# More and narrower filler products, and a new order of all steps, in a fused attention and gated MLP kernel

## The chip, the cores and the metric

The kernel runs on one core of a Trainium2 chip. The metric is the device time of one execution in microseconds; several executions are timed and their median is given. One more execution is recorded by the hardware profiler, and every row shown here comes from that one.

## The reference

For 8 batches of 576 tokens and 8 heads of 64, attention keeps only the scores within `tau` of the row's maximum; the 8 heads are then joined to 512 columns and pass a gated MLP whose gate mixes tokens.

```python
scores = scale * np.matmul(q, k.transpose(0, 1, 3, 2))
thresh = np.max(scores, axis=-1, keepdims=True) - tau
scores = np.where(scores >= thresh, scores, -1000000000.0)
attn = np.exp(scores - np.max(scores, axis=-1, keepdims=True))
attn = attn / (np.sum(attn, axis=-1, keepdims=True) + 1e-09)
x = (attn @ v)                      # heads side by side: (B, S, 512)
...
h = gelu_tanh(x @ w_in)             # (B, S, 1024)
u, v = h[..., :512], h[..., 512:]
v_n = (v - mean(v)) / np.sqrt(var(v) + 1e-06) * g_ln
v_s = np.einsum('ts,bsd->btd', w_sg, v_n) + b_sg[None, :, None]
return x + (u * v_s) @ w_out
```

## The kernel before

The work is cut into 32 attention units `n` (a batch and two heads each; four units make a batch) and 8 MLP units. All inputs are float32; the MLP's products are made of high and low parts, three products for each, so TensorE (PE) has most of the work.

An attention unit loads `rq`, `rk` and `rv`, scales `rq` on GpSimd (POOL), and makes scores for four blocks of 128 queries and a tail of 64 (`scores`, 16 PE records for a block; `tail_scores`). A block fills two pairs of PSUM banks, one for each head. VectorE (DVE) takes the row maximum, POOL the threshold, ScalarE (ACT) the selection (`select`, which frees the banks) and the exponential (`exponentials`); DVE transposes blocks of 32 (`turn_blocks`), and DMAs issued by SyncE (SP) write them to DRAM tiles `swa` and `swb` and read them back into `pt` (`put_blocks`, `get_blocks`). PE then multiplies by `rv` (`values`), and the result becomes `x`. Once a batch has its four `x` tiles, its MLP runs between the attention of the units that follow.

The first batch has no MLP of an earlier batch beside it. In this opening the weights are also prepared: the words of `w_in` and `w_out` come as float64 and are turned into high and low parts by ACT, POOL, DVE and, for six of them, PE (`rest`, three products with 512 columns).

Each step of all this is entered into a list, `plan`. What the engines get is `plan` in the order of the table `ORDER`, a list of step numbers that is written out in the file. Every engine then works through its own instructions in that order. `PLACES` is a second table: one digit for each request of PSUM banks, in the order of the requests.

`warm_up` is a step without use for the result: it multiplies a tile of ones by itself into a PSUM bank that nobody reads.

Of the kernel before, what the change touches and what calls it, by code (L numbers as in the profile page):

```python
# [12 lines left out]
F32 = mybir.dt.float32  # L13
# [18 lines left out]
    172 16 17 173 18 174 65 250 7 1 14 71 188 19 178 189 190 66 191 76 179 180 67 176 68 195 192 69 181 175 196 182  # L32
    204 70 206 205 193 183 185 77 12 4 194 197 207 72 251 211 214 98 208 252 87 215 216 253 217 78 73 224 186 209 184
    225 5 221 218 74 266 79 226 187 10 88 212 54 80 227 75 222 99 213 267 210 9 15 219 268 223 228 89 100 32 21 220 43
    139 198 150 229 82 256 236 269 273 270 257 258 282 55 199 90 259 81 200 237 91 177 238 44 263 328 283 83 254 101
    284 260 231 285 274 203 230 46 84 93 286 232 289 261 292 239 330 329 85 102 293 92 294 201 302 332 295 103 303 262
    202 271 299 275 86 234 233 94 235 13 3 109 296 241 300 406 264 304 95 331 240 297 305 272 334 96 45 244 104 306
    245 242 128 49 335 336 265 56 97 287 337 338 290 11 105 6 344 341 307 298 301 291 243 339 276 278 22 60 407 112
    110 106 288 277 246 346 345 409 107 408 314 308 247 38 360 347 248 249 281 309 362 361 47 310 280 315 255 57 348
    351 380 8 349 363 108 316 340 381 317 342 350 382 113 367 370 383 364 343 352 371 372 279 412 410 114 373 111 353  # L40
    313 115 312 33 374 413 377 414 415 320 58 422 311 355 318 416 375 368 116 384 419 118 321 59 378 365 423 48 424
    117 425 61 322 376 323 369 739 385 379 426 366 319 2 324 62 35 417 420 429 325 50 741 354 356 134 392 121 448 421
    450 449 327 51 27 393 386 451 388 326 34 119 394 455 418 452 387 52 458 430 124 427 456 358 459 333 460 438 359
    395 120 428 440 740 24 156 461 125 0 439 441 23 357 431 122 36 445 442 63 126 37 390 462 446 25 389 745 746 391
    747 432 26 123 748 400 396 397 398 749 443 742 399 453 743 752 28 39 463 457 401 447 444 127 755 151 64 454 29 40
    470 402 434 433 153 145 756 753 152 757 53 129 464 403 471 30 140 758 466 762 791 465 41 759 405 404 31 771 472
    154 772 411 773 42 437 155 131 130 792 435 774 473 501 750 778 436 760 467 761 793 468 775 142 794 484 781 469 132
    776 133 475 474 795 478 476 783 763 782 157 477 764 479 784 502 583 135 785 788 754 751 779 136 141 789 158 780
    786 480 817 518 481 485 787 796 161 482 159 160 790 137 803 584 486 777 503 487 895 488 765 767 766 20 504 505 489
    490 506 804 818 491 492 138 493 567 519 568 520 507 494 534 819 495 521 522 496 483 508 509 523 497 510 535 823  # L50
    799 797 591 511 498 162 536 575 499 824 825 512 826 744 770 513 514 143 805 500 827 515 830 592 537 524 164 585
    525 768 769 569 833 526 538 798 516 806 800 527 810 539 576 550 528 529 586 834 835 517 570 809 540 551 577 530
    144 541 167 531 836 163 828 571 532 533 837 165 572 840 802 801 552 553 573 896 146 542 543 554 807 811 574 899
    544 578 545 587 555 808 812 588 599 556 546 557 813 558 147 559 613 589 841 822 579 580 849 547 831 148 560 820
    614 590 561 581 548 851 582 593 562 600 897 838 850 594 563 606 549 821 839 852 595 596 853 856 601 615 607 608
    829 832 898 564 597 859 565 598 842 566 844 843 634 860 861 635 854 814 609 857 616 862 845 636 610 617 866 602
    863 858 855 869 603 815 149 637 870 867 901 871 864 902 620 903 621 166 872 904 873 638 865 622 908 627 905 623
    628 816 624 629 847 618 630 639 604 874 973 848 975 168 169 605 868 911 912 913 170 611 914 641 881 882 642 883
    648 906 649 612 846 877 875 650 876 640 631 625 643 884 918 880 915 619 626 907 651 171 927 632 655 652 633 929
    656 662 919 916 644 878 653 928 654 657 909 658 663 664 887 879 910 930 974 947 917 931 934 886 937 920 948 645  # L60
    976 977 949 923 665 939 888 938 935 676 666 885 659 677 950 940 921 667 646 941 944 1300 889 936 979 647 890 945
    932 942 668 922 981 980 946 678 933 697 982 660 983 986 951 989 891 943 1025 892 679 926 1302 952 900 990 991 698
    690 893 984 987 699 1026 691 985 992 1027 993 996 1028 959 988 894 661 953 700 955 1005 960 692 997 683 1029 994
    954 961 701 925 924 1007 1006 680 1301 1008 684 669 962 670 671 693 1009 995 998 1012 958 681 1304 1015 1010 694
    672 957 967 956 1016 1017 999 966 1013 1000 1018 704 1303 685 1001 1014 1030 686 702 1019 1022 968 963 1306 965
# [989 lines left out]
```

## Time and profile before

| | |
|---|---|
| median of 3 executions | 855.63 us |
| the three | 855.70, 855.63, 844.68 us |
| the profiled execution | 844.72 us, its span 842.9 us |
| granted TensorE clock, mean over the span | 0.996 of full |
| busy share | PE 96%, ACT 77%, DVE 74%, POOL 57% |

The span runs from the first to the last instruction; 1.8 us of the profiled execution lie around it. Busy time of PE is modelled, since its products overlap. A granted clock of 1.0 is the 2.4 GHz level, 0.5 the 1.2 GHz level.

### The profile page before, as it was taken

How to read it: one execution, taken by the hardware profiler on the slowest of the kernel's cores; microseconds unless marked ns; L12 is line 12 of the kernel's file. 1: busy time of each engine (PE TensorE's matmuls, PEld its weight loads, DVE VectorE, ACT ScalarE, POOL GpSimd, SP SyncE). 2: the span in 40 equal slices, each digit the busy share in tenths (PEclk: the TensorE clock that was granted, in tenths of full speed). 3: DMA queues.
4: the chain of work that ended last, by engine and by line, in shares of the span. 5: the costliest groups of instructions: out<-in, count | busy, mean ns of one | idle time of the engine just before them, and what ended most of it. 6: DMA issues, size and time to landing. Idle time of an engine off the chain costs nothing.

```text
span 842.9 us, 24738 instructions
## 1 busy us (share of the span) xinstructions
PE 808.5 (96%) x9726; PEld 661.7 (78%) x9726; DVE 625.0 (74%) x1118; ACT 644.8 (77%) x1358; POOL 479.8 (57%) x809
## 2 busy tenths in 40 slices
PE   7779989999999999999999999999999999999898
PEld 4445767887888778888888878878788878889798
DVE  6888788858878487875788678874987748876265
ACT  6988879858979488786888678884898759886271
POOL 4788798544754477254753557334665348435283
PEclk9999999999999999999999999999999999999999
DMA  7998865784678735996558836797377853877402
GB/s 283 261 278 225 230 154 144 203 231 136 147 205 223 188 105 153 239 247 151 149 160 221 228 100 132 212 255 208 109 186 203 215 144 94 210 198 188 106 8 71
DMA packets 218998, 151.74 MB, mean 180 GB/s; under 512 B 32257, under 2 KB 204289, under 8 KB 218882
## 3 DMA queue, kind: packets, MB, share of 16 engines
q1 hardware_dynamic: 218882, 150.16, 67.0%
q8 instruction: 76, 1.25, 0.6%
q14 instruction: 40, 0.33, 0.1%
HBM read 97.68 MB, written 52.43 MB: 178 GB/s over the span
## 4 chain that ended last, share of the span: by engine, by line
PE 55%; DMA 16%; POOL 9%; SPq 6%; DVE 5%; ACT 5%; issue 3%; DVEq 0%; POOLq 0%; ACTq 0%
PE all_banks L759 33%; PE all_banks L552 11%; PE all_banks L667 9%; DMA pt<-swb 4%; DMA swb<-pt 4%; PE all_banks L559 2%; DMA ir<-ird 2%; SPq L646 2%; DVE pt L636 2%; SPq L653 2%; DVE columns L568 2%; DMA swa<-pt 2%; DMA rq<-in_qT 1%; DMA out_T<-ot 1%; ACT p L582 1%
## 5 line engine op out<-in xcount | busy, mean ns | idle before, releaser
L568 DVE TENSOR_REDUCE columns<-all_banks 128x1 f32<-128x576 f32 x288 | 205.6, 748 | 69.2 <-PE all_banks L552 48.7
L582 ACT ACTIVATE p<-all_banks,columns 128x576 f32<-128x576 f32 x288 | 201.5, 736 | 58.4 <-POOL columns L572 57.9
L588 ACT ACTIVATE p<-p,columns 128x576 f32<-128x576 f32 x288 | 221.0, 772 | 0.9
L636 DVE STREAM_TRANSPOSE pt<-p 128x576 f32<-128x576 f32 x288 | 209.0, 756 | 13.1 <-ACT p L588 7.6
L552 PE MATMUL all_banks<-rk,rq 64*64 64x288 f32 x2048 | 167.1, 417 | 11.5 <-ACT p L582 8.6
L667 PE MATMUL all_banks<-pt,rv 64*64 64x128 f32 (+1 forms) x4608 | 156.0, 284 | 7.8 <-DMA pt<-swb 4.3
L667 PEld LDWEIGHTS all_banks<-pt,rv 64*64 64x64 f32 x4608 | 144.7, 133 | 18.3 <-DMA pt<-swb 5.1
L572 POOL TENSOR_TENSOR columns<-columns 128x2 f32<-128x2 f32 (+1 forms) x160 | 34.1, 213 | 173.0 <-DVE columns L568 160.9
L552 PEld LDWEIGHTS all_banks<-rk,rq 64*64 64x64 f32 x2048 | 77.9, 133 | 64.3 <-ACT p L582 23.3
L759 PE MATMUL all_banks<-x,wi 128*128 128x288 f32 (+2 forms) x720 | 114.6, 300 | 0.0
L759 PE MATMUL all_banks<-wi,x 128*128 128x512 f32 (+1 forms) x424 | 110.4, 398 | 3.7 <-ACT ot L976 2.8
L759 PE MATMUL all_banks<-wsh,z 128*128 128x288 f32 (+2 forms) x512 | 112.2, 302 | 0.6 <-POOL z L880 0.6
L967 POOL TENSOR_TENSOR ot<-ot,x 128x288 f32<-128x288 f32 x112 | 89.9, 805 | 39.5 <-ACT ot L976 34.7
L759 PEld LDWEIGHTS all_banks<-x,wi 128*128 128x128 f32 x720 | 101.1, 188 | 13.6 <-issue 9.2
L759 PE MATMUL all_banks<-gh,wo 128*128 128x288 f32 (+1 forms) x480 | 107.7, 301 | 1.4 <-DVE ir L677 1.2
L759 PEld LDWEIGHTS all_banks<-wi,x 128*128 128x128 f32 (+1 forms) x424 | 74.2, 184 | 23.6 <-ACT ot L976 3.0
L759 PEld LDWEIGHTS all_banks<-wsh,z 128*128 128x128 f32 x512 | 83.4, 188 | 11.1 <-issue 6.4
L759 PEld LDWEIGHTS all_banks<-gh,wo 128*128 128x128 f32 x480 | 79.5, 188 | 14.5 <-issue 5.3
L759 PE MATMUL all_banks<-wsl,z 128*128 128x288 f32 (+2 forms) x256 | 74.4, 299 | 0.0
L685 POOL TENSOR_TENSOR x<-ir,x 128x576 fp32r<-128x576 f32 x32 | 45.6, 1424 | 42.8 <-ACT x L682 39.2
L759 PE MATMUL all_banks<-gl,wo 128*128 128x288 f32 (+1 forms) x240 | 69.7, 295 | 0.0
L675 DVE TENSOR_TENSOR ir<-all_banks,ir 128x512 f32<-128x512 f32 x32 | 21.7, 677 | 50.6 <-PE all_banks L667 38.8
(163 smaller groups left out, 1151.5 us busy)
## 6 DMA issues: line engine op xcount, KB each, us to landing
rv<-in_vP SPq DMA_DIRECT2D x32, 576.0 KB, 5.4
swb<-pt SPq DMA_DIRECT2D x64, 180.0 KB, 3.9
swb<-pt SPq DMA_DIRECT2D x32, 360.0 KB, 4.0
pt<-swb SPq DMA_DIRECT2D x64, 180.0 KB, 4.8
pt<-swb SPq DMA_DIRECT2D x32, 360.0 KB, 5.7
rq<-in_qT SPq DMA_DIRECT2D x32, 288.0 KB, 4.5
rk<-in_kT SPq DMA_DIRECT2D x32, 288.0 KB, 4.2
swa<-pt SPq DMA_DIRECT2D x32, 288.0 KB, 3.9
```

The lines of the kernel that those rows point to most:

```text
L552: nc.tensor.matmul(st["s", h, i][cols, a, 0:HALF], st["q"][rows, i * P + c * D:i * P + (c + 1) * D], st["k"][rows, a * HALF:(a + 1) * HALF ...
L559: nc.tensor.matmul(sc[:, a, 0:HALF], tails[part], st["k"][:, a * HALF:(a + 1) * HALF], start=True, stop=True)
L568: return lambda: nc.vector.tensor_reduce(nm, st["s", h, i][:, :, 0:HALF], AX.XY, ALU.max, negate=True)
L572: return lambda: nc.gpsimd.tensor_tensor(nt, nm, toff[:, 0:1] if i == NM else toff, ALU.subtract)
L582: nc.scalar.activation(halves(st["p", h, i]), st["s", h, i][:, :, 0:HALF], AF.Prelu, bias=columns_of(i)[1][:, h:h + 1], alpha=BIG)
L588: return lambda: nc.scalar.activation(st["p", h, i], st["p", h, i], AF.Exp, bias=toff[:, 0:1], accum_out=l_of[part][:, c:c + 1])
L636: nc.vector.transpose(out, st["p", h, i].rearrange("p (j x) -> p j x", x=BLK))
L667: nc.tensor.matmul(st["acc"][h * D:(h + 1) * D, r, :, c0:c0 + w], v[rows, c, h], x[:, :, h * w:(h + 1) * w], start=(c == 0), stop=(c == PA ...
L675: nc.vector.tensor_tensor(main, acc[:, :, 0:MAINQ], main, ALU.mult)
L685: nc.gpsimd.tensor_tensor(xl_of[b, hp], st["ir"], xh_of[b, hp], ALU.subtract)
L759: nc.tensor.matmul(st["acc"][0:rows[0]] if rows else st["acc"], w, x, start=(j == 0), stop=(j == n - 1))
L967: return lambda: nc.gpsimd.tensor_tensor(o(), o(), x[b, m][:, ts_], ALU.add)
```

## The change

`WARM = 48` filler products are entered in place of 16, and 39 of the 48 stand in `ORDER`. Each has 128 columns in place of 256. They write the last 128 columns of a bank, where scores (columns 0 to 287 of a bank) have none. The tile of ones is 128 columns wide. `ORDER` and `PLACES` are new from the first entry to the last; since 32 more entries stand at the head of `plan`, the number of every later step is also higher by 32.

```diff
+    WARM = 48
...
-    warm = mtmp.tile([P, FH], F32, tag="mt1", name="warm")[:, 0:256]
+    warm = mtmp.tile([P, FH], F32, tag="mt1", name="warm")[:, 0:P]
     nc.vector.memset(warm, 1.0)
 
     def warm_up(i):
-        return lambda: nc.tensor.matmul(bank(f"warm{i}")[:, 0:256], warm[:, 0:P], warm, start=True, stop=True)
-
-    for i in range(16):
+        return lambda: nc.tensor.matmul(all_banks[:, bank_of(1), 512 - P:512], warm, warm, start=True, stop=True)
+
+    for i in range(WARM):
         at("warm", i, warm_up(i))
...
 ORDER = [int(i) for i in """
-    172 16 17 173 18 174 65 250 7 1 14 71 188 19 178 189 190 66 191 76 179 180 67 176 68 195 192 69 181 175 196 182
...
```

What the tables move is seen in the engines' own order. A row is an instruction, what it writes and reads, the output's shape and how often it follows itself. The numbers behind the names only tell buffers apart.

PE, from its first product to the tail scores of unit 0, before (`rk_131`, `rq_125` are unit 0's):

```order
L994 MATMUL all_banks<-warm 128x256 x3
L552 MATMUL all_banks<-rk_131,rq_125 64x288 x24
L994 MATMUL all_banks<-warm 128x256 x2
L552 MATMUL all_banks<-rk_131,rq_125 64x288 x8
L559 MATMUL all_banks<-rk_131,tails_110 128x288 x2
L994 MATMUL all_banks<-warm 128x256
```

The same place now (`rk_133`, `rq_125` are unit 0's):

```order
L996 MATMUL all_banks<-warm 128x128 x9
L554 MATMUL all_banks<-rk_133,rq_125 64x288 x8
L996 MATMUL all_banks<-warm 128x128 x2
L554 MATMUL all_banks<-rk_133,rq_125 64x288 x8
L996 MATMUL all_banks<-warm 128x128
L554 MATMUL all_banks<-rk_133,rq_125 64x288 x8
L996 MATMUL all_banks<-warm 128x128 x3
L554 MATMUL all_banks<-rk_133,rq_125 64x288 x8
L996 MATMUL all_banks<-warm 128x128 x2
L561 MATMUL all_banks<-rk_133,tails_110 128x288 x2
L996 MATMUL all_banks<-warm 128x128 x5
```

Three fillers of 256 columns before the first scores became nine of 128, and one to three stand between the score blocks, where three blocks stood in a row.

PE, from the first weight's products to the tail scores of unit 1, before (`rk_220` is unit 1's; `ident_r` and `minus` mark a weight's products):

```order
L430 MATMUL all_banks<-wt1h,ident_r 128x512
L430 MATMUL all_banks<-wt1l,ident_r 128x512
L430 MATMUL all_banks<-wi_229,minus 128x512
L552 MATMUL all_banks<-rk_220,rq_135 64x288 x8
L994 MATMUL all_banks<-warm 128x256 x3
L552 MATMUL all_banks<-rk_220,rq_135 64x288 x24
L430 MATMUL all_banks<-wt_196,ident_r 128x512 x2
L430 MATMUL all_banks<-wi_355,minus 128x512
L559 MATMUL all_banks<-rk_220,tails_111 128x288 x2
```

The same place now (`rk_164` is unit 1's, `wt1h` to `wi_272` the first weight's):

```order
L554 MATMUL all_banks<-rk_164,rq_195 64x288 x8
L996 MATMUL all_banks<-warm 128x128 x2
L432 MATMUL all_banks<-wt1h,ident_r 128x512
L432 MATMUL all_banks<-wt1l,ident_r 128x512
L432 MATMUL all_banks<-wi_272,minus 128x512
L996 MATMUL all_banks<-warm 128x128 x2
L554 MATMUL all_banks<-rk_164,rq_195 64x288 x8
L996 MATMUL all_banks<-warm 128x128 x4
L554 MATMUL all_banks<-rk_164,rq_195 64x288 x16
L561 MATMUL all_banks<-rk_164,tails_111 128x288 x2
L996 MATMUL all_banks<-warm 128x128
```

Unit 1's first block now stands ahead of the first weight's products, fillers stand on both sides of these and behind the second block, and the second weight's products have moved behind the tail.

SP, from the write of unit 0's sums to the loads of unit 3, before (`rq_411` is unit 3's `rq`):

```order
L606 DMA ird_372<-ir_333 128x32
L520 DMA rk_374<-in_kT 128x576
L653 DMA pt_0_200<-swa_292 64x9x128
L653 DMA pt_0_200<-swa_292 32x9x128
L653 DMA pt_0_271<-swb_348 32x9x160
L653 DMA pt_0_271<-swb_348 64x9x160
L653 DMA pt_0_271<-swb_348 32x9x160
L463 DMA wt_405<-in_w_sgT 128x576
L618 DMA ir_333<-ird_372 64x4x16
L520 DMA rq_411<-in_qT 128x576
L611 DMA ir_333<-ird_372 64x4x128 x2
```

The same place now (`rk_422` and `rq_434` are unit 3's):

```order
L608 DMA ird_360<-ir_345 128x32
L522 DMA rk_364<-in_kT 128x576
L655 DMA pt_0_252<-swa_263 64x9x128
L655 DMA pt_0_252<-swa_263 32x9x128 x2
L655 DMA pt_0_320<-swb_341 32x9x160
L655 DMA pt_0_320<-swb_341 64x9x160
L655 DMA pt_0_320<-swb_341 32x9x160
L522 DMA rk_422<-in_kT 128x576
L613 DMA ir_345<-ird_360 64x4x128 x2
L522 DMA rq_434<-in_qT 128x576
L387 DMA raw_wo_444<-in_w_out 128x1024
L620 DMA ir_345<-ird_360 64x4x16 x2
```

Unit 3's `rk` is now issued ahead of its `rq`, both ahead of the tail part of the sums' reads, and the load `wt_405` of a weight no longer stands between.

## Rows read from the trace of the kernel before

**Rows 1.** The page: the span, busy time of the engines, and their busy tenths in 40 slices.

```profile
span 842.9 us, 24738 instructions
...
PE 808.5 (96%) x9726; PEld 661.7 (78%) x9726; DVE 625.0 (74%) x1118; ACT 644.8 (77%) x1358; POOL 479.8 (57%) x809
...
PE   7779989999999999999999999999999999999898
```

**Rows 2.** Windows: length, busy us (count) by engine, PE clock, DMA share, GB/s.

```profile
6.30:11.30 5.00, 3.07 (x38) 1.70 (x42) 2.75 (x4) 2.79 (x5) 1.51 (x4) 1.00 1.01 401
11.30:14.70 3.40, 3.40 (x18) 1.67 (x10) 2.73 (x5) 3.40 (x9) 1.14 (x4) 0.50 1.03 410
14.70:28.30 13.60, 10.65 (x83) 5.32 (x82) 12.95 (x22) 13.56 (x28) 8.62 (x16) 1.00 0.82 265
28.30:31.70 3.40, 3.40 (x17) 1.69 (x18) 2.11 (x4) 3.40 (x7) 3.23 (x7) 0.51 1.03 258
...
90.00:842.90 752.90, 735.01 (x8901) 617.59 (x8899) 554.94 (x1000) 570.55 (x1209) 414.69 (x701) 1.00 0.65 170
```

**Rows 3.** Timeline of PE, 0 to 70 us: start, length, instructions, idle before and releaser.

```profile
1.21 2.93 PE L994 MATMUL all_banks<-warm 128*128 128x256 f32 x6 [1.21 <-DVE warm L991]
6.31 2.17 PE L552 MATMUL all_banks<-rk,rq 64*64 64x288 f32 x32 [2.18 <-DMA rk<-in_kT]
10.40 2.57 PE L552 MATMUL all_banks<-rk,rq 64*64 64x288 f32 x16 [1.92 <-ACT p L582]
12.90 2.02 PE L994 MATMUL all_banks<-warm 128*128 128x256 f32 x4
14.85 1.20 PE L552 MATMUL all_banks<-rk,rq 64*64 64x288 f32 x16
...
20.80 1.56 PE L994 MATMUL all_banks<-warm 128*128 128x256 f32 x6
22.30 1.20 PE L552 MATMUL all_banks<-rk,rq 64*64 64x288 f32 x16
25.87 1.82 PE L552 MATMUL all_banks<-rk,rq 64*64 64x288 f32 x16 [2.37 <-ACT p L582]
...
47.93 1.24 PE L559 MATMUL all_banks<-rk,tails 128*128 128x288 f32 x4 [1.55 <-ACT p L582]
...
63.16 0.70 PE L994 MATMUL all_banks<-warm 128*128 128x256 f32 x2
```

**Rows 4.** Timeline of ACT, 0 to 45 us, the first work and the second wait.

```profile
8.52 0.67 ACT L419 ACTIVATE raw_wi<-raw_wi 128x512 f32<-128x512 uint32 x1 [6.51 <-DMA raw_wi<-in_w_in]
...
9.63 1.34 ACT L582 ACTIVATE p<-all_banks,columns 128x576 f32<-128x576 f32 x2
...
24.36 0.67 ACT L419 ACTIVATE raw_wi<-raw_wi 128x512 f32<-128x512 uint32 x1
```

**Rows 5.** Timeline of DVE, 0 to 30 us, round the first scores.

```profile
7.55 2.75 DVE L568 TENSOR_REDUCE columns<-all_banks 128x1 f32<-128x576 f32 x4 [1.63 <-PE all_banks L552]
...
16.10 1.42 DVE L568 TENSOR_REDUCE columns<-all_banks 128x1 f32<-128x576 f32 x2 [0.24 <-PE all_banks L552]
```

**Rows 6.** Chain that ended last, 0 to 100 us, in order of time: start, length.

```profile
10.40 2.57 PE all_banks L552 x16
12.97 1.95 PE all_banks L994 x4
...
22.39 4.20 DMA swa<-pt
...
36.31 6.10 DMA rq<-in_qT
...
78.36 2.56 POOL wz L420 x2
```

**Rows 7.** Timeline of PE, 764 to 800 us: the longest late wait and a late stretch.

```profile
784.09 2.11 PE L759 MATMUL all_banks<-wi,x 128*128 128x512 f32 x8 [2.78 <-ACT ot L976]
...
796.01 3.04 PE L759 MATMUL all_banks<-x,wi 128*128 128x256 f32 x24
```

More of the change, by code (lines that the diff above doesn't have):

```diff
@@ L31 @@
 ORDER = [int(i) for i in """
[194 rows of a table removed]
[195 rows of a table added]
 """.split()]
 PLACES = "".join("""
-    0102046024546201640002046024655420456420644062406424604277024027462076024745677025601246721642074206241642712406
-    0246024724062401426142067412642645260126456201624562062346024620752042064207642062476402704263740064014623416430
-    4620614526026540256023064364026401241640216426423064520640645607340267402604526426072401624260462540620652602346
-    0326406413426246041562026054123560246430642067402360430646020645026740260426430140642461426704270423064506206752
-    0472047602542064023604236406432046126426742064712460452376043064206460452640526012646214264520462023674524060124
-    73510632754730216716
+    0101010102045642204544623201010046767726454004260454442604266024544600264024016402406420620456026754230437360472
+    4062453605026401261426704264023064206306423604502360206236045063206540632060467340763407204640236402640204650262
+    0456023460260274012460724601452260426702640234072042602414267024702402745602306206230156264152601267406024360450
+    6250623460246420742012407642046724020427450267502470123746242062460234601246124642024562062460421646024264526046
+    2015260462360456062012467142674023042642016240164245602304670604304234064124567014214260462641236403640124624162
+    1402614620145670124237516041326450176321046
 """.split())
```

388 rows, old and new, of the table ORDER are left out of this document.

## The prediction

> **What bounds the kernel now.** I read the page first, then windows, PE's timeline and the chain of waits. PE is busy for 808.5 of 842.9 us [rows 1], so at most 34.4 us of PE's waits can be won. The windows split them: after 90 us PE is busy for 735.0 of 752.9 us, which leaves 17.9 us of waits in many small pieces; the first 90 us hold the other 73.4 us of PE's work and 16.6 us of waits [rows 1, 2]. After the opening PE is the bound. In the opening it is not: ACT is busy for 13.56 of 13.60 us between 14.7 and 28.3 us, while PE waits, and the longest of these waits, 2.37 us, ends when ACT has emptied a score bank [rows 2, 3].
>
> The clock is the second thing to see. It fell to 0.50, the 1.2 GHz level, at about 11.3 us and at 28.3 us, and stood there some 3 us each time [rows 2]. Ahead of the first fall lie PE waits of 2.18 and 1.92 us, ahead of the second one of 2.37 us; a wait of 1.55 us later, at 47.9 us, did not bring one [rows 3]. At the low level 16 score records took 2.57 us, at the high level 1.20 us; two fillers of 256 columns took 1.95 us from start to start against 0.50 us each (20.80 to 22.30 us for three) [rows 3]. The first three fillers took 2.93 us, so they ran at the low level too [rows 3].
>
> **What the fillers cost.** The sixteen took 2.93 us (three), 1.95 us (two) and eleven times 0.50 us, so 10.4 us of PE [rows 3]. One of 128 columns isn't in the trace. By columns it is half of 0.50, so 0.25 us; from above, it is bounded by a 256-column one, 0.50 us. Weight loads need not hold it up: 24 records of 256 columns with 128x128 weights passed in 3.04 us, 0.13 us each, and a filler is two records (six for three) [rows 3, 7]. I take 0.25 us, and 0.49 us at the low level. The first nine then run from 1.21 to 5.6 us, and the first scores started at 6.31 us, when `rk` had landed [rows 3]: they cost nothing, because the load hides them; if `rk` came in time for 5.6 us they would still cost nothing. The other thirty take 7.5 us where thirteen took 7.45 us (1.95 + 5.5): no difference in sum. At 0.50 us each they would take 15 us, 7.5 us more, the upper end.
>
> **What lies on the path.** The chain runs through PE from 10.40 us: a score block of 2.57 us and two fillers of 1.95 us, then the next block [rows 6]. All of that is at the low level. At the high level, with the three fillers that now stand there, it is 1.20 + 0.75 us in place of 4.52 us: 2.6 us less. I expect the clock to stay up here, since both waits ahead of it shrink: the first from 2.18 to 0.7 us (fillers end at 5.6 us), the second to about 1.4 us (the two new fillers between unit 0's blocks put the second block's end from 8.48 to about 9.0 us, against 10.40 us, when ACT frees the bank) [rows 3]. The new fillers delay nothing there: ACT takes up its first work only at 8.52 us, when a weight has landed, and DVE's first maximum reads the first block alone [rows 4, 5].
>
> Not all of the 2.6 us arrives. ACT was busy for 3.40 of the 3.40 us and DVE for 2.73 of them [rows 2], and DVE had waited only 0.24 us when the next maxima came [rows 5]: what PE saves is worth at least DVE's 0.67 us of idle time there. Between 0.67 and 2.6 us I take 1.2 us, nearer the lower, since ACT had no gap at all.
>
> The second fall I expect to stay, or to move by a few us. PE then waits for ACT's selection of unit 1's first blocks, and ACT does as many exponentials and weight steps ahead of it as before; it had just done a weight step at 24.36 us [rows 4]. The four fillers that now stand ahead of unit 1's third block are, by the digits of `PLACES`, in the banks of these same blocks, so they wait with it. The weight's products, which now stand behind unit 1's first block, fill no more than they did. It costs nothing either way: the chain is in DMAs there, from 22.39 us, and then in the load of a `rq` from 36.31 us [rows 6].
>
> **The other queues.** SP issues unit 3's loads with one weight load less ahead of them; its `rk` is now first and its `rq` comes two reads later. The `rq` of 6.10 us was on the chain [rows 6], but SP issues cost about as much before as behind it. I put this at nothing, with 0.7 us either way, DVE's idle time above being the nearest slack that a row shows. POOL's weight work is the same sum in another order, and it is POOL that the chain follows at 78.36 us [rows 6], so what is won at 10 us can still be lost there: another reason for the low 1.2 us. From 90 us on I count by hand: with PE's pieces at their pitch, the work between a unit's last scores and the second half of its values is the same in both orders within 3 us, unit by unit. So I take 0 for the rest. Its bounds are half of the 17.9 us won or as much again lost, 9 us either way.
>
> **Sum.** The profiled execution took 844.7 us, its span and 1.8 us around it. Less 1.2 us that gives 843.5 us. The median of 855.6 us is another matter: two of the three executions lie 10.9 us above the third, which is the level of the profiled one. No row shows how the longer ones went.
>
> **Rivals.** *Two levels stay.* If the 10.9 us come from something that the fillers don't touch (transfers, say), two executions in three may lie high again: 855.6 - 1.2 = 854.4 us. For it: the half-speed stretches that the trace shows are 6.8 us [rows 2] and 2.93 us at the start [rows 3], and half of 9.7 us is 4.9 us, not 10.9 us. Against it: the opening is where a clock can fall at all, and other executions may fall more often. The Trainium skill's page "TensorE: Matmul & The Clock Gate" (Part 1, "What's actually happening") puts the penalty of the slow start below 1% of a typical span, and says that the number of slow products differs from run to run; no run here shows a second execution's clock. By that rule the clock would give at most 8.4 us of the 10.9 us, and the levels would stay apart by the rest, about 847 us at the best.
>
> *The fillers don't fill.* Where a filler's bank still holds scores it waits for the same selection as the block behind it. Then both falls stay, and the time is the profiled one, 844.7 us. For it: most new fillers stand in such banks. Against it: the first eleven do not. The skill's page "PSUM — Partial Sum Buffer" ("PSUM bank collisions raise a hardware error") asks that waits go by bank and not by address; then columns 384 to 511 are no freer than the scores' own. No row of before shows it, since a filler of 256 columns overlaps the scores anyway.
>
> *Slower.* The fillers stand ahead of scores, and PE works in order. If the clock falls early and stays low, thirty fillers cost 14.7 us in place of 7.45 us, and each of the sixteen score blocks of units 0 to 3 costs 1.37 us more (2.57 - 1.20 us [rows 3]): 7.3 + 21.9 = 29 us at most, so 873 us. It decides from the point where it costs more than ACT's time hides; with 12 us of it the time is 857 us. Against it: both falls had ended by 14.7 and 31.7 us [rows 2].
>
> *Faster in the rest.* The new order wins half of the waits after 90 us, among them the single one of 2.78 us at 784 us [rows 7]: 843.5 - 9 = 834.5 us.
>
> **How the numbers follow.** Forecast (839 to 846 us) 0.40; fillers don't fill (844 to 848 us) 0.15; two levels stay (851 to 857 us) 0.24; faster in the rest (832 to 838.5 us) 0.10; slower (857 to 873 us) 0.11. The likeliest is 843.5 us. The range from 837 to 857 us leaves out the last two but for 0.02. A change of 2% is about what a measurement of this kernel can tell from none; that is 838.5 and 872.7 us about the median of 855.6 us. Below lies the case of the rest, 0.10; above only the end of the slower case, 0.03; between them 0.87.
>
> **What would show it.** Right: nine first fillers of about 0.49 us and the first scores at 6.3 us; no low clock between 10 and 16 us; the third score block in about 1.2 us; a low stretch between 23 and 33 us; the first fillers in banks with scores starting just behind a selection of ACT; PE's waits after 90 us near 18 us. Wrong: a clock that is low for more than 7 us in the opening; fillers longer than 0.3 us at the high level; PE's waits after 90 us off by more than 5 us. The forecast would be wrong above all if the three executions again split into two levels.

## The result, and the profile after

The changed kernel took 858.76 us (median of 4 executions, 854.51 to 864.20) against 852.42 us (844.68 to 855.70, 4 executions) of the kernel before on the same chip: a ratio of 1.0108, 95% interval 1.0061 to 1.0154. Forecast were 843.5 us and a range of 837 to 857 us, so the time lies above the range, by 1.8 us. A ratio, here and below, leaves out executions that are over 1.5% above the fastest of their kernel, and differs by up to 0.3% from the quotient of the two medians, which count all. The profiled execution took 857.28 us, its span 855.5 us. All rows below are from it, unless a sentence says otherwise. Line numbers in it are higher by 2: L554 are the scores, L669 the values, L761 the MLP's products, L996 the fillers.

The page first, with the span, the busy times, and PE's busy tenths and clock in 40 slices, which answer to [rows 1]:

```profile
span 855.5 us, 24846 instructions
...
PE 817.3 (96%) x9772; PEld 666.3 (78%) x9772; DVE 629.2 (74%) x1118; ACT 644.4 (75%) x1358; POOL 481.7 (56%) x809
...
PE   7878999999999999999999989999999989999998
...
PEclk9999999999999989999999999999999999999999
```

The span is 12.6 us longer, and 8.8 us of that are PE's busy time (817.3 against 808.5 us). PE was idle for 38.2 us, where it had been for 34.4 us. So two thirds of the longer span count as busy time of PE, and one third as waits; the slice in which the clock fell is the fifteenth, far behind the opening.

The windows of [rows 2], then three more that split the time behind 90 us: length, busy us (count) by engine, PE clock, DMA share, GB/s.

```profile
6.30:11.30 5.00, 3.89 (x28) 2.19 (x32) 1.42 (x2) 1.22 (x2) 0.14 (x1) 1.00 1.03 407
11.30:14.70 3.40, 3.40 (x34) 1.44 (x26) 1.42 (x2) 2.71 (x6) 0.87 (x3) 1.00 1.02 405
14.70:28.30 13.60, 11.60 (x91) 7.25 (x88) 12.86 (x20) 13.35 (x28) 7.58 (x16) 1.00 0.71 232
28.30:31.70 3.40, 2.54 (x26) 1.40 (x25) 2.97 (x7) 3.40 (x8) 1.38 (x4) 1.00 0.78 221
...
90.00:843.00 753.00, 733.52 (x8853) 610.32 (x8852) 554.59 (x993) 571.37 (x1213) 417.60 (x703) 1.00 0.65 170
...
90.00:300.00 210.00, 202.66 (x2565) 165.22 (x2563) 157.90 (x284) 162.09 (x346) 123.34 (x203) 1.00 0.71 186
300.00:307.00 7.00, 5.87 (x13) 4.23 (x14) 5.57 (x9) 3.57 (x6) 4.36 (x8) 0.52 0.40 100
307.00:855.50 548.50, 534.40 (x6347) 450.08 (x6346) 395.78 (x712) 405.71 (x862) 291.24 (x494) 1.00 0.62 163
```

Both stretches of the opening at half clock are gone from the clock's column (1.00 where 0.50 and 0.51 stood), and a new one stands at 300 us, in the middle of the MLP's products. From 90 us to the end of the span PE was busy for 742.9 of 765.5 us (the last three rows together), which leaves 22.6 us of waits, 4.7 us more than before (17.9 us). As far as 843 us they are 19.5 us, but the span goes on for 12.5 us there.

PE's timeline (start, length, instructions, idle before and releaser) of the places of [rows 3], of the new low stretch, and of the late stretch of [rows 7]:

```profile
1.07 4.21 PE L996 MATMUL all_banks<-warm 128*128 128x128 f32 x18 [1.07 <-DVE warm L993]
7.41 2.20 PE L554 MATMUL all_banks<-rk,rq 64*64 64x288 f32 x16 [2.13 <-DMA rk<-in_kT]
9.54 1.22 PE L996 MATMUL all_banks<-warm 128*128 128x128 f32 x4
10.69 2.20 PE L554 MATMUL all_banks<-rk,rq 64*64 64x288 f32 x16
12.82 0.80 PE L996 MATMUL all_banks<-warm 128*128 128x128 f32 x2
13.55 1.20 PE L554 MATMUL all_banks<-rk,rq 64*64 64x288 f32 x16
15.47 0.94 PE L996 MATMUL all_banks<-warm 128*128 128x128 f32 x6 [0.73 <-ACT p L584]
...
19.34 1.28 PE L996 MATMUL all_banks<-warm 128*128 128x128 f32 x10
20.55 1.99 PE L554 MATMUL all_banks<-rk,rq 64*64 64x288 f32 x16
...
28.03 1.16 PE L996 MATMUL all_banks<-warm 128*128 128x128 f32 x8 [0.90 <-ACT p L584]
29.12 1.20 PE L554 MATMUL all_banks<-rk,rq 64*64 64x288 f32 x16
31.18 1.83 PE L554 MATMUL all_banks<-rk,rq 64*64 64x288 f32 x16 [0.86 <-ACT p L584]
...
300.80 1.22 PE L761 MATMUL all_banks<-wi,x 128*128 128x512 f32 x2 [2.39 <-ACT x L684]
302.35 5.42 PE L761 MATMUL all_banks<-wi,x 128*128 128x512 f32 x13 [0.33 <-POOL x L687]
...
799.08 3.13 PE L669 MATMUL all_banks<-pt,rv 64*64 64x160 f32 x72 [0.34 <-DMA pt<-swb]
```

Nine fillers took 4.21 us, 0.47 us each; five took 1.21 us from start to start (19.34 to 20.55 us), 0.24 us each. The first two score blocks took 2.20 us each and the third 1.20 us: by these lengths PE ran at the 1.2 GHz level as far as 13.5 us, though the clock's column gives 1.00 there (the same holds of the first fillers in [rows 3]). The first scores, which wait for `rk`, started at 7.41 us, not at 6.31 us. The single late wait of 2.78 us [rows 7] isn't there any more, and a wait of 2.39 us for an MLP's `x` ends at 300.80 us; the clock falls in it, at 300.2 us, and stays at half for 6.8 us. There 13 of the MLP's products took 5.42 us.

The answers to [rows 4] and [rows 5] are ACT's first work on scores and DVE's first maxima, from their timelines:

```profile
11.39 1.37 ACT L584 ACTIVATE p<-all_banks,columns 128x576 f32<-128x576 f32 x2 [1.44 <-POOL columns L574]
...
14.68 1.37 ACT L584 ACTIVATE p<-all_banks,columns 128x576 f32<-128x576 f32 x2 [0.60 <-POOL columns L574]
```

```profile
9.65 1.42 DVE L570 TENSOR_REDUCE columns<-all_banks 128x1 f32<-128x576 f32 x2 [4.29 <-PE all_banks L554]
12.94 1.42 DVE L570 TENSOR_REDUCE columns<-all_banks 128x1 f32<-128x576 f32 x2 [1.87 <-PE all_banks L554]
```

ACT began its first selection at 11.39 us (9.63 before), and DVE waited 1.87 us for the second block. The chain of waits shows the same, in order of time, for [rows 6]:

```profile
1.63 5.65 DMA rk<-in_kT
7.41 2.20 PE all_banks L554 x16
9.61 1.15 PE all_banks L996 x4
10.76 2.13 PE all_banks L554 x16
...
35.25 6.25 DMA pt<-swb
41.52 6.71 DMA ir<-ird
```

The rows offer two theories. **Theory 1**: the opening lost the time (slow first blocks, 23 more fillers on PE), and the rest only carries it on. **Theory 2**: the new order of the rest lost it, where the prediction had put 0.

### The profile page after: what moved, and what is told of

It is laid out like the page before. It is cut to its first block, busy times and chain, and to the rows that moved or that the text cites. A ratio compares the mean times of both kernels' runs of the same rounds, so it can differ in the third digit from the quotient of the medians.

```text
span 855.5 us, 24846 instructions
## 1 busy us (share of the span) xinstructions
PE 817.3 (96%) x9772; PEld 666.3 (78%) x9772; DVE 629.2 (74%) x1118; ACT 644.4 (75%) x1358; POOL 481.7 (56%) x809
## 4 chain that ended last, share of the span: by engine, by line
PE 59%; DMA 13%; POOL 8%; ACT 7%; DVE 6%; issue 3%; SPq 3%; POOLq 0%; DVEq 0%; ACTq 0%
PE all_banks L761 35%; PE all_banks L554 11%; PE all_banks L669 9%; DMA ir<-ird 3%; PE all_banks L561 3%; DMA ird<-ir 3%; DMA pt<-swb 3%; ACT p L584 2%; DVE columns L570 2%; DMA out_T<-ot 2%; ACT p L590 2%; DMA swb<-pt 2%; POOL x L687 1%; DVE pt L638 1%; SPq L655 1%
## 5 line engine op out<-in xcount | busy, mean ns | idle before, releaser
L554 PE MATMUL all_banks<-rk,rq 64*64 64x288 f32 x2048 | 166.0, 418 | 8.6 <-ACT p L584 3.7
L669 PE MATMUL all_banks<-pt,rv 64*64 64x128 f32 (+1 forms) x4608 | 156.0, 284 | 9.7 <-DMA pt<-swb 4.2
L669 PEld LDWEIGHTS all_banks<-pt,rv 64*64 64x64 f32 x4608 | 144.5, 133 | 22.1 <-issue 7.1
L554 PEld LDWEIGHTS all_banks<-rk,rq 64*64 64x64 f32 x2048 | 75.4, 133 | 58.6 <-issue 13.5
L761 PE MATMUL all_banks<-wi,x 128*128 128x512 f32 (+1 forms) x424 | 114.3, 407 | 4.8 <-ACT x L684 2.4
L761 PE MATMUL all_banks<-wsh,z 128*128 128x288 f32 (+2 forms) x512 | 114.1, 304 | 2.3 <-DVE uu L740 1.0
L761 PE MATMUL all_banks<-x,wi 128*128 128x288 f32 (+2 forms) x720 | 114.3, 299 | 0.0
L761 PEld LDWEIGHTS all_banks<-x,wi 128*128 128x128 f32 x720 | 101.2, 188 | 10.8 <-issue 7.2
L761 PE MATMUL all_banks<-gh,wo 128*128 128x288 f32 (+1 forms) x480 | 106.5, 300 | 0.0
L761 PEld LDWEIGHTS all_banks<-wi,x 128*128 128x128 f32 (+1 forms) x424 | 76.0, 188 | 28.8 <-issue 3.9
L761 PEld LDWEIGHTS all_banks<-wsh,z 128*128 128x128 f32 x512 | 83.8, 188 | 13.8 <-issue 6.9
L761 PEld LDWEIGHTS all_banks<-gh,wo 128*128 128x128 f32 x480 | 79.2, 188 | 12.4 <-issue 6.6
L761 PE MATMUL all_banks<-wsl,z 128*128 128x288 f32 (+2 forms) x256 | 74.1, 296 | 0.0
L761 PE MATMUL all_banks<-gl,wo 128*128 128x288 f32 (+1 forms) x240 | 70.1, 298 | 0.0
L590 ACT ACTIVATION_READ_ACCUMULATOR p<-p,columns 128x1 f32 x288 | 56.5, 196 | 0.0
```

Source lines behind the costliest of these rows:

```text
L554: nc.tensor.matmul(st["s", h, i][cols, a, 0:HALF], st["q"][rows, i * P + c * D:i * P + (c + 1) * D], st["k"][rows, a * HALF:(a + 1) * HALF ...
L590: return lambda: nc.scalar.activation(st["p", h, i], st["p", h, i], AF.Exp, bias=toff[:, 0:1], accum_out=l_of[part][:, c:c + 1])
L669: nc.tensor.matmul(st["acc"][h * D:(h + 1) * D, r, :, c0:c0 + w], v[rows, c, h], x[:, :, h * w:(h + 1) * w], start=(c == 0), stop=(c == PA ...
L761: nc.tensor.matmul(st["acc"][0:rows[0]] if rows else st["acc"], w, x, start=(j == 0), stop=(j == n - 1))
```

## The experiments

The two orders hold the same steps but for fillers. At each cut used below (behind the second half of a unit's `values`; the expectations call it the unit's values or first values) they have also done the same steps but for fewer than 20, so that one order can be continued by the other. The table of such a kernel is made like this, with `new` and `old` for the tables of after and before and `k` for the cut; each step keeps its banks' digits where they are free. Fillers come from the first piece alone.

```diff
-ORDER = new
+ORDER = new[:k] + [s for s in old if s not in new[:k]]
```

Every ratio is to the kernel before on the same chip, with its 95% interval. In the five sets of these runs, each on another chip and of 23 to 31 executions, that kernel's medians were 847.5, 848.2, 848.8, 848.9 and 851.5 us, its single times 840.9 to 859.1 us (one of 3445 us left out).

**The opening or the rest.** Four kernels: the changed one again; the new order as far as unit 3 (532 steps), the old one behind it; the opposite; and the changed order with 20 fillers of 256 columns in place of the 39 of 128.

```diff
-    warm = mtmp.tile([P, FH], F32, tag="mt1", name="warm")[:, 0:P]
+    warm = mtmp.tile([P, FH], F32, tag="mt1", name="warm")[:, 0:256]
...
-        return lambda: nc.tensor.matmul(all_banks[:, bank_of(1), 512 - P:512], warm, warm, start=True, stop=True)
+        return lambda: nc.tensor.matmul(all_banks[:, bank_of(1), 0:256], warm[:, 0:P], warm, start=True, stop=True)
```

> The changed kernel once more, unchanged, to narrow its ratio. If the loss is fixed in the program (opening or rest of the order), the ratio to the kernel before stays near 1.011, and the profile again has units' value products 3 to 5 us late in the opening and about 10 us late from unit 12 on. If it was chance (one low stretch of the clock at 300 us, which costs about 3.4 us plus a wait of 2.4 us), the stretch is missing here and the ratio falls to about 1.004.

> The new order, with its 39 fillers, up to the values of unit 3 (the first 532 steps), then all other steps in the order of before. Theory 1 (the opening loses: it runs at the low clock until 13.5 us and makes every unit 3 to 5 us late): ratio 1.004 to 1.006, that is 3 to 5 us. Theory 2 (the rest of the new order loses, through waits such as the one of 2.4 us at 300 us and the low clock behind it): ratio 1.000 to 1.002.

> The order of before, with its 16 fillers of 256 columns, up to the values of unit 3 (494 steps), then all other steps in the new order. Theory 1 (opening): ratio 1.000 to 1.003. Theory 2 (rest): ratio 1.007 to 1.010, and a wait of PE for the x tile of unit 11 near 295 us with a low clock behind it. If both hold, the two spliced kernels' losses add up to that of the changed kernel.

> The new order throughout, but each two of its 39 fillers of 128 columns are one of 256 (20 in all, five at the start). If narrow fillers are the reason that the clock stayed low until 13.5 us, it is high by about 4.5 us here as in the kernel before, the fillers take about 2.9 us less and the ratio is 0.003 to 0.004 below that of the changed kernel. If the clock's rise hangs on when the fillers fall and not on their width, or the rest of the order is what loses, the ratio is that of the changed kernel within 0.002.

| kernel | median us, executions | ratio |
|---|---|---|
| changed, again | 854.51, 12 | 1.0068 (1.0035 to 1.0102) |
| new opening, old rest | 849.85, 12 | 1.0015 (0.9980 to 1.0050) |
| old opening, new rest | 858.73, 6 | 1.0109 (1.0050 to 1.0167) |
| new order, wide fillers | 858.54, 12 | 1.0112 (1.0076 to 1.0148) |

Theory 1 falls as an account of the loss: with the new opening alone the time can't be told from that of before (its interval holds a loss of up to 0.5%, though), and with the new rest alone the loss is all there. It is even greater than that of the changed kernel on the same chip, by 4.2 us of the medians, so the two parts don't add up. In the new order, 20 wide fillers did worse than 39 narrow ones, by 4.0 us of the medians; both forecasts for them missed, a gain of 0.3 to 0.4% and no change within 0.2%.

The new low stretch at 300 us isn't what makes the loss either. In the profile of the changed kernel's second run, the waits at that place are shorter and the same 13 products took 3.24 us in place of 5.42 us; the clock was half at 8.3, 73.2 and 574.9 us instead, and 5.7 us of loss stayed (854.51 against 848.80 us). PE's timeline of it:

```profile
298.18 0.73 PE L761 MATMUL all_banks<-wi,x 128*128 128x512 f32 x2 [0.82 <-ACT x L684]
299.73 3.24 PE L761 MATMUL all_banks<-wi,x 128*128 128x512 f32 x13 [0.82 <-POOL x L687]
...
800.66 1.21 PE L761 MATMUL all_banks<-x,wi 128*128 128x256 f32 x8 [1.65 <-ACT ot L978]
```

**Two places.** In the two profiles of the changed kernel PE took longer than in that of before at two places, between units 9 and 12 (with the waits for `x` near 300 us) and at the end, behind unit 31. The wait for `ot` near 800 us is in the second profile alone, and the kernel before has one of 2.78 us for `ot` at 784 us [rows 7]. **Theory 3**: these two places hold the loss, some 3 us each. The other view (rival 4 in the expectations) is many small pieces. Repaired were the end (new order as far as unit 31, old one behind), units 9 to 12 (old order between these cuts) and both; and the new piece of units 9 to 12 was put into the old order. The edits are the splice above with these cuts.

```diff
-ORDER = old
+ORDER = old[:k9] + [s for s in new[:k12] if s not in old[:k9]]
+ORDER += [s for s in old if s not in ORDER]
```

> The new order up to the values of unit 31, then the order of before for the rest (the last batch's MLP; 16 of 603 bank places differ from either table). Theory 3 (two places of the rest lose: the stretch from unit 9 to 12, where the profiles show 3.3 us more beyond PE's usual pitch, and the end behind unit 31, 3.0 us): 3 us below the changed kernel, ratio 1.003 to 1.004 against 1.007 for the changed one. Rival 4 (the loss lies in many small pieces): within 1 us of the changed kernel, or above it because of the seam.

> The new order, but the steps between the values of unit 9 and of unit 12 in the order of before, then the new order again. Theory 3: 3 us below the changed kernel, ratio 1.003 to 1.004, and no wait of PE for the x tile of unit 11 behind its values. Rival 4: ratio 1.006 to 1.010.

> Both replacements at once: units 9 to 12 and the end in the order of before, all else new, 39 fillers. Theory 3: 6 us below the changed kernel, ratio 1.000 within 0.003. Rival 4: no better than 1.005.

> The order and the fillers of before, with only the steps between the values of unit 9 and of unit 12 in the new order. Theory 3: 3 us above the kernel before, ratio 1.003 to 1.004, and PE waits for the x tile of unit 11. Rival 4: ratio 1.000 within 0.002.

| kernel | median us, executions | ratio |
|---|---|---|
| new, old end | 855.50, 12 | 1.0069 (1.0043 to 1.0096) |
| new, old units 9 to 12 | 855.79, 10 | 1.0068 (1.0036 to 1.0100) |
| new, both repairs | 857.15, 8 | 1.0093 (1.0044 to 1.0143) |
| old, new units 9 to 12 | 858.73, 6 | 1.0102 (1.0058 to 1.0147) |

Theory 3 doesn't hold as it was put. Both repairs together were to give 1.000 within 0.003 and gave 1.0093; the new piece in the old order was to cost 0.3 to 0.4% and cost 1.0%, which rival 4 missed too (1.000). The single repairs were to gain 3 us; they show no gain over the 1.0068 of the changed kernel, but that was measured on another chip, and by the two intervals a gain of 3 us isn't excluded. The repairs do what they should at their place: with the old piece of units 9 to 12, the profile has no wait ahead of a product of `wi` and `x` between 288 and 321 us, and with the old end alone no wait for `ot` near 800 us (with both repairs one of 1.99 us stands there again). PE's timeline of the old order with the new piece has waits for `x` there (L758 are the MLP's products), and ahead of them one for ACT's selection (L581):

```profile
270.17 0.40 PE L758 MATMUL all_banks<-wsh,z 128*128 128x288 f32 x1 [2.52 <-ACT p L581]
...
300.99 3.24 PE L758 MATMUL all_banks<-wi,x 128*128 128x512 f32 x13 [0.52 <-POOL x L684]
```

**The fillers.** The kernel before once more, with 32 fillers of 128 columns in place of its 16 of 256, and with none; and the new order with none.

```diff
-    for i in range(16):
+    for i in range(WARM):
```

The line above belongs to the narrow ones, with the tile and the columns of the change; without fillers their entries are taken out of `ORDER` and nothing else.

> The kernel before against itself. Ratio 1.000 within 0.004. If the first profile of it (span 842.9 us) was one of its faster executions, as its other times suggest, this one's span is 845 to 850 us and its waits lie in other places than those of the first; theory 3 then rested on too fast a picture of before.

> The order of before; each filler of 256 columns is two of 128 at the same place (32). Theory 5 (narrow fillers keep the clock up better: the new openings had a mean clock of 0.9966 to 0.9977, the old ones 0.991 to 0.995): clock 0.9965 or more and ratio 0.997 to 0.999. Rival (it is where the fillers stand): clock 0.995 as before, ratio 1.000 within 0.003.

> The order of before without any filler. If fillers are worth their time, the clock is low for 10 us or more in the opening (mean clock 0.990 or less) and the ratio 1.003 to 1.008. If ACT and the transfers bound the opening whatever PE does, ratio 1.000 within 0.003.

> The new order without any filler. If the loss of the new order is in its other steps, the ratio is at least that of the changed kernel (1.007 to 1.011), and higher by what the fillers are worth. If the 39 fillers delay the opening, it falls to 1.003 or less.

| kernel | median us, executions | ratio |
|---|---|---|
| before, again | 848.22, 12 | 1.0013 (0.9986 to 1.0040) |
| old order, 32 narrow fillers | 849.03, 12 | 1.0004 (0.9978 to 1.0030) |
| old order, no fillers | 852.39, 12 | 1.0040 (1.0015 to 1.0064) |
| new order, no fillers | 859.59, 6 | 1.0117 (1.0079 to 1.0155) |

The second profile of the kernel before has a span of 846.4 us, as forecast, and other waits than the first: the one of 2.78 us at 784 us isn't in it. Fillers are worth 0.4% (3.4 us) in the old order. That is as much as the mean clock loses without them: 0.9918 against 0.9958 of the kernel before on that chip. In the new order the narrow ones are worth about as much (1.0117 against 1.0068, on different chips), the wide ones nothing that shows (1.0117 against 1.0112); why isn't shown. In the old order narrow ones in twice the number do no better than wide ones, and their mean clock was 0.9949, not the 0.9965 of the second expectation's theory 5, which is a theory of the fillers and not the theory 5 below. Without any filler the new order is still 0.8% slower than the old one (859.59 against 852.39 us on one chip), so the loss is in the order of the other steps.

**A place for the loss.** The program was cut at unit 12 and at unit 20, both ways. **Theory 4** puts the loss ahead of unit 12, **theory 5** spreads it evenly and lets the pieces add up, **theory 6** says that any departure from the old order costs the same.

> The new order (its 39 narrow fillers with it) as far as the first values of unit 12, the old order of the steps behind it. If the loss lies ahead of unit 12 (theory 4): 1.007 times the kernel before, and the run with the opposite halves 1.000. If it is spread evenly over units 3 to 31 (theory 5), 9 of 28 units give 1.0025 here and 1.0055 in the opposite run. If any departure from the old order costs about the same, wherever it is (theory 6): 1.007 in all four runs.

> The old order (its 16 wide fillers with it) as far as the first values of unit 12, the new order behind it. Theory 4 (loss ahead of unit 12): 1.000. Theory 5 (spread): 1.0055. Theory 6 (any departure costs): 1.007.

> The new order as far as the first values of unit 20, the old one behind it. Theory 4 (loss ahead of unit 12): 1.007. Theory 5 (spread): 17 of 28 units, 1.005. Theory 6 (any departure costs): 1.007. A loss that lies behind unit 20: 1.000.

> The old order as far as the first values of unit 20, the new one behind it. Theory 4 (loss ahead of unit 12): 1.000. Theory 5 (spread): 11 of 28 units, 1.003. Theory 6 (any departure costs): 1.007. A loss that lies behind unit 20: 1.007.

Then two short pieces in the old order, by the second splice with other cuts:

> The old order and its 16 wide fillers, with the new order's steps only from unit 12's to unit 15's first values. If any departure from the old order costs about the same (theory 6): 1.006 to 1.009. If pieces add up to the whole loss (theory 5), 3 of 28 units are worth 0.1%: 1.001, and the piece of units 9 to 12, at 1.010, was a special one.

> The same with the new order's steps only from unit 25's to unit 28's first values. Theory 6 (any departure costs): 1.006 to 1.009. Theory 5 (pieces add up): 1.001.

| kernel | median us, executions | ratio |
|---|---|---|
| new as far as unit 12, then old | 855.89, 9 | 1.0088 (1.0053 to 1.0122) |
| old as far as unit 12, then new | 855.91, 12 | 1.0083 (1.0053 to 1.0112) |
| new as far as unit 20, then old | 853.87, 12 | 1.0057 (1.0025 to 1.0088) |
| old as far as unit 20, then new | 853.71, 12 | 1.0059 (1.0027 to 1.0091) |
| old, new units 12 to 15 | 849.03, 12 | 1.0018 (0.9989 to 1.0046) |
| old, new units 25 to 28 | 849.35, 12 | 1.0011 (0.9982 to 1.0041) |

Theory 4 falls with the second row: the new order behind unit 12 costs 0.8% alone. Theory 6 falls with the last two: a short piece can cost next to nothing. Theory 5 has the short pieces right (0.1% forecast) and the halves at unit 20 nearly (0.5 and 0.3%), but the halves at unit 12 add up to 1.7%, and units 9 to 12 alone cost 1.0%. The cuts themselves needn't cost anything: the last two kernels have two each. So loss lies behind unit 3 in more than one stretch, and in these times the stretches don't add up.

**What it is made of.** The profiles of these runs can be put together. Taken was, for each PE record from unit 3's first value product on, the distance to the next record's start, less the median distance of its kind in the trace of before; the fillers are left out. Scores and values go in pairs or fours with 0.007 us between them, and that is their median, so most of the sums below is their usual pitch; what counts is the difference. Seven profiles have the old order there (with at most a piece of three units exchanged), six the new one (with the old end in one).

```
                                              old    new   difference, us
sum over the rest                           259.6  264.2   +4.6
  in stretches at half clock                  0.9    1.8   +0.9
  distances longer by over 0.3 us            52.4   54.3   +1.9
    ahead of wi,x                             6.0    9.3   +3.2
    ahead of rk,rq                            3.9    5.7   +1.8
    ahead of pt,rv                            8.7   10.1   +1.4
    ahead of x,wi                            10.5    8.4   -2.1
    ahead of gh,wo and tails                 12.3    9.2   -3.2
  all others                                                +1.8
```

From one profile to another the sum differs by 2.2 us (old) and 3.0 us (new, one standard deviation), and one of the new ones lies at 258.2 us, below the old mean; the difference of 4.6 us has a standard error of some 1.6 us. The same sum for the opening, with the fillers counted whole, is 65.6 us in the nine profiles with the old opening and fillers and 66.4 us in the nine with the new one: +0.8 us. Cut behind the last of unit 3's value products, the two differences are 3.7 and 2.2 us. Together 5.4 us (5.9 us by the other cut), near to what the timings of the changed kernel's second run give (854.51 - 848.80 = 5.7 us).

Whether it shows as idle time can be read from windows. The kernel before in its second run, then the changed one in its second run: length, busy us (count) for PE, PEld, DVE, ACT, POOL, then PE clock, DMA share, GB/s.

```profile
0.00:90.00 90.00, 73.89 (x827) 43.75 (x828) 70.05 (x119) 74.42 (x149) 65.28 (x109) 0.98 0.94 263
90.00:300.00 210.00, 204.12 (x2578) 167.20 (x2577) 161.64 (x289) 165.46 (x351) 126.07 (x206) 1.00 0.69 182
300.00:780.00 480.00, 468.65 (x5798) 392.12 (x5799) 363.22 (x647) 380.22 (x808) 254.80 (x449) 1.00 0.67 178
780.00:860.00 80.00, 61.84 (x528) 57.87 (x526) 29.31 (x65) 24.59 (x51) 33.64 (x46) 1.00 0.20 56
```

```profile
0.00:90.00 90.00, 74.15 (x850) 46.51 (x850) 70.61 (x115) 73.28 (x147) 62.77 (x106) 0.96 0.88 248
90.00:300.00 210.00, 203.13 (x2568) 165.93 (x2567) 160.44 (x287) 162.93 (x347) 124.95 (x206) 1.00 0.72 186
300.00:780.00 480.00, 470.19 (x5733) 389.81 (x5732) 362.63 (x646) 380.54 (x808) 256.66 (x452) 1.00 0.67 177
780.00:860.00 80.00, 68.55 (x632) 63.95 (x624) 35.96 (x72) 28.20 (x58) 37.29 (x49) 0.99 0.24 68
```

At 780 us 632 PE records are left in the changed kernel, 528 in the one before: 6.7 us of PE's work (68.55 - 61.84). PE had been busy in the 480 us ahead of that for 1.5 us more, and done 65 records less. It wasn't idle; its records there were longer in the mean, in part because they are another mix of shapes. So the lag doesn't show as idle time here: over the span PE was idle for 38.0 us in the changed kernel and 37.9 us in the one before.

When it arose these counts don't tell, since value products follow each other at 0.03 us in the mean and products of `wi,x` at 0.24 us. The end of a unit's values does: at the cuts named below both orders have done the same PE work within 0.6 us. There the changed kernel is later, in these two profiles, by 5.1 us at unit 3, 3.8 us at unit 9, 4.9 us at unit 12, 6.7 us at unit 20 and 4.6 us at unit 31, and by 7.6 us at the last record.

Read like this, all 20 profiles give the pieces a length in either order, whatever stands ahead of them:

| piece, between the ends of units' values | new less old, us | standard error, us |
|---|---|---|
| start to unit 3 (17 profiles: left out are those without fillers and the new order with wide ones) | +2.2 | 0.7 |
| units 3 to 9 | +0.2 | 0.5 |
| units 9 to 12 | +1.9 | 0.8 |
| units 12 to 31 | -0.6 | 1.3 |
| unit 31 to the end | +2.9 | 0.8 |

The sum is 6.6 us. So in the profiles the loss has three places, two of which are those of theory 3, and the opening is the third. The times of the repairs don't show the gain that follows from it (2.9, 1.9 and 4.8 us), and the piece of units 9 to 12 cost more in the old order than 1.9 us. A profile is one execution and a time the median of 6 to 12; which of the two misleads isn't shown.

## Why the prediction was wrong

**The step that failed** is "From 90 us on I count by hand ... So I take 0 for the rest". The count was of PE's work between a unit's last scores and its values; the two orders hold the same steps, so the work in all is indeed the same. What the count didn't hold are the distances between the records. They cost 4.6 us by the profiles and 0.7 to 1.1% (6 to 9 us) by the runs with a new rest, which is inside the bounds of 9 us either way that stood beside it, but on the side that was not taken. Shown is that the rest does it (new opening with old rest 1.0015, old opening with new rest 1.0109); not shown is which of its exchanged steps. The sign that was to catch it, PE's waits behind 90 us, didn't: they were 22.6 us, 4.7 us above the 17.9 us of before, and the sign asked for more than 5 us. The longer distances count as busy time of PE for the most part, and the profile of before had the fewest such waits of the seven with the old rest (17.9 to 24.9 us; 19.9 to 26.6 us in the six with the new one).

**The base was mis-sized as well.** "Less 1.2 us that gives 843.5 us" starts from the profiled 844.7 us as one of two levels. No two levels show: the 135 executions of the five sets lie between 840.9 and 859.1 us, in each set without a gap of more than 3.8 us, and the profiled execution was one of the faster. With 852.4 us of the same chip as the base, 7.7 us of the miss of 15.3 us are this term, 6.3 us the measured difference, and 1.2 us the gain that didn't come. The rival of two levels came within 4.4 us (854.4 us) by a mechanism that the sets don't show, so that was luck.

**The opening** is the second step that failed: "Between 0.67 and 2.6 us I take 1.2 us". Right: a full-speed filler costs 0.24 us (0.25 forecast), a slow one 0.47 us (0.49), and the first nine were hidden, since the scores, which wait for `rk`, started 2.13 us behind them. Right: the clock's column shows no fall between 10 and 16 us, and the third block took 1.20 us. Wrong: the first two blocks were slow (2.20 us each), and two slow fillers stood between them, 1.15 us; what was saved behind 10 us was lost ahead of it, and ACT's first selection came 1.76 us later. That this varies with the execution is seen in the other profiles: by the lengths of the records, the first full-speed record came between 4.0 and 13.5 us with the new opening, and between 6.2 and 15.4 us with the old one and its fillers. The second fall near 28 us didn't come in this profile; the wait of 2.37 us had become one of 0.90 us ahead of fillers and one of 0.86 us ahead of the next block. Of the 1.2 us forecast nothing arrived: a loss of 0.8 or 2.2 us by the profiles, by where unit 3 is cut, and 1.0015 by the run, whose interval (-1.7 to +4.2 us) holds gain and loss. It isn't that the clock fell as often as before: by the clock's column, which doesn't show the slow first records, the seven kernels with the new opening and narrow fillers had mean clocks of 0.9962 to 0.9978, those with the old opening and its fillers 0.9910 to 0.9958. What that saved on PE didn't come through as time.

**The rivals.** "The fillers don't fill" had its mechanism right, though not its time (844.7 us) or its two falls: fillers in banks that still held scores waited for the selection, 0.73 us at 15.47 us and 0.90 us at 28.03 us. The rule by which it was argued, in the Trainium skill's page "PSUM — Partial Sum Buffer" ("PSUM bank collisions raise a hardware error"), to guard by bank and not by address, is what these rows agree with. "Slower" had the range right (857 to 873 us) and the place wrong: it put the loss into a low clock among the fillers. The loss stayed without any filler. "Faster in the rest" named the wait of 2.78 us at 784 us, which did go; others came in its place, and the second profile of the kernel before doesn't have it either. The argument against two levels, that "the opening is where a clock can fall at all", is wrong by the fall at 300.2 us. The steps of SP and POOL can't be told apart from the opening's sum.

The fillers as a whole were worth 0.4%. The Trainium skill's page "TensorE: Matmul & The Clock Gate" ("What's actually happening") puts the penalty of the slow start below 1% of a typical span. The 0.4% lies below that, but it is what the fillers win, and no run here shows what the slow start costs in all.

**What stays open** is why the rest is slower. By the table of distances, waits ahead of `wi,x`, scores and values grew by 6.4 us (the 1.4 us of the values aren't clear of their standard error of 1.1 us), those ahead of `x,wi`, `gh,wo` and tails shrank by 5.3 us, and the rest is small change over thousands of records. That pieces of the new order cost 1.0% (units 9 to 12) or 0.1% (units 25 to 28) alone, and that taking the costly one out of the new order shows no gain, is measured; it would fit that a delay in one stretch is made up or passed on by the slack of the next, but no run separates that from chance in how two orders meet at a cut. No version beat the kernel before.

## What to carry to other kernels

Where an engine is busy for 96% of the span, a new order of its steps is judged by the distances between its records and not by the amount of work; an estimate of 0 with bounds says that nothing is known, and the range must then be laid about the centre of many executions and not about the one that was profiled. Before blaming the place where a trace shows a new wait, look at a second profile of the same kernel, and repair that place alone: here the waits of one place were taken out (2.7 us in one profile, 1.6 us in the next), and no gain showed. To find where time is lost, compare when the same work is done, not how many records are left. An edit with two parts (fillers and order) is taken apart first, since one may pay and the other cost more.

## What the runs showed of the hardware

The clock fell to half not only in the opening but in stretches where PE is the bound: at 300.2 us for 6.8 us in a wait of 2.39 us in one execution of the changed kernel, at 574.9 us for 3.4 us behind one of 1.69 us in the next. Late falls stood at such waits in other profiles too: at 804.0 us behind a wait of 3.32 us (old opening, new rest), at 803.4 us behind one of 2.87 us (old as far as unit 12). The wait alone doesn't decide: behind the one of 2.78 us at 784 us in the profile of before [rows 7] the clock's column shows no fall. Of the 19 waits of PE of more than 1.9 us behind 90 us in the 20 profiles, nine have a fall at them and ten have none.

The spread between executions goes with the clock in part only. In the five sets of the kernel before, the correlation of the time with the clock's loss was 0.61, 0.54, 0.22, 0.70 and -0.10. The mean clock of the changed kernel's second run was 0.9968 and that of before on the same chip 0.9951: it had the better clock, and was slower.
